# Gated complex attention and GEGLU on one core: more transposes by DMA, unread matmuls, float32 sums in the first units, wider gate blocks

## The chip, the cores and the metric

The kernel runs on one core of a Trainium2 chip. Its engines are TensorE (PE), VectorE (DVE), ScalarE (ACT), GpSimd (POOL) and SyncE (SP), which here only issues transfers. The metric is the device time of one execution in microseconds. A profile is one execution taken by the hardware profiler, and its time is a little longer than the median of the runs without it.

## The reference, cut to what matters

Inputs `q`, `k`, `v`, `a_re`, `a_im` have 4 batches, 8 heads, 768 positions and 48 elements. The first half is a linear attention whose state decays by a complex gate per position and element; the second half is a gated feed-forward block over 3072 tokens of 384 elements (8 heads x 48), with 1536 hidden elements.

```python
mag = np.sqrt(a_re * a_re + a_im * a_im)
scale = np.minimum(mag, 0.999) / (mag + 1e-06)
for t in range(S):
    new_re = ar * S_re - ai * S_im
    new_im = ar * S_im + ai * S_re
    S_re, S_im = (new_re + outer(k[t], v[t]), new_im)
    y[t] = q[t] @ S_re
x = y of all heads, 3072 x 384
val = x @ w_val;  gelu = GELU(x @ w_gate)
out = x + sigmoid(x @ w_res) * ((gelu * val) @ w_out)
```

The kernel does not step through the positions. It takes logarithm and angle of the gate, sums both over the 128 positions of a tile with a triangular matrix on PE, scales q by the exponential of the sum and k by its inverse, and turns both by cosine and sine of the summed angle. Scores inside a tile are then plain matmuls under a mask, and what comes from earlier tiles goes through a state of 96 x 48 a head.

## The kernel before, in words

**Units.** A tile is 128 positions of one batch, with all 8 heads. The 24 tiles are grouped into 14 units (lines 211 to 217): units 0 and 1 are one tile each, units 2 to 11 two tiles each, and units 12 and 13 one tile each. Unit 2 holds the first tiles of batches 2 and 3; from unit 3 on, two units take each next position tile of batches 0, 1 and 2, 3.

**Steps.** `prepare` (L364), `attend` (L512) and `forward` (L577) do not run anything; each adds steps to a plan, 1450 of them. `Plan.run` (L158) then issues them in the order of the hand-given list `ORDER` (an index per step), so that list sets the order on every engine's queue. Each engine works its own queue strictly in that order. `PLACE` says for steps that may run on several engines which one takes them. Buffers are given out in the same order: a step whose buffer is still in use waits for the last user. Where ACT changes between the tables for logarithm and exponential (L), for arctangent and sine (T) and for GELU and tanh (G), a table load is put in (L652). Steps of DVE and POOL that share a port wait for one another in turn (L179 to L183).

**Prepare, for one unit.** SP loads `ar`, `ai`, `q`, `k`, `vf` (L373), a transfer for each tile. ACT takes Ln of `ar` into `la` (L394) and Exp of its negative into `t` (L395); `t` times `ai` (L397) is the tangent; its square (L399 or L401) goes through Ln again (L402), and L403 joins both into the log magnitude. L406 caps it and rounds it to the short float format `lh`, L408 makes the rest `ll`; `sums` (L359) adds both up on PE with two matmuls into a bank, and ACT takes E and Ei, the exponentials of the sum and of its negative (L423, L424). ACT takes the arctangent (L433), the carry of the tile before is added by a DMA of POOL (L440, L446), `th` and `tl` are its two parts (L450, L452), summed by `sums` as well; ACT rounds the number of turns (L462) and DVE takes them off (L464). `fw` is the absolute value (L471 or L473), and two sines fill `CS` (L477). L482 scales q and k, L487 makes the features `fQ`, `fK` of 128 x 8 x 128. They are then transposed to `QT`, `KT`: in units 0 to 7 on PE (L504, eight matmuls against the identity for each tile and each of Q and K), with a copy out of the bank by DVE or ACT (L507); in units 8 to 13 (`PE_T = 8`) by a transposing DMA of SP (L496). L510 casts `v`.

**Attend.** Scores (L535), mask (L538), the product with v and the state (L547, L549), the copy `x` (L552), and the new state: L559, U (L565), Gb (L567) and Gf (L572).

**Forward.** `x` is transposed (on PE in units 0 to 2, L591; by DMA later, L583). For each pair of the 12 hidden blocks of 128, PE fills one bank with gate products and one with value products (L605); ACT takes the GELU of the gate bank (L610), and DVE multiplies it with the value bank (L611). A block of a unit with two tiles is 256 wide, so two blocks are 512 elements and fill a bank; in a unit of one tile, two blocks are 256 and fill half of it. L620 and L622 make the residual gate, L631 the output product, L635 and L638 the result, L640 the store.

**Memory.** PE writes into eight banks, all of one kind (`Bank`). The wide float32 buffers are a pool of 25 (`WD`), of which each unit takes 16: five loads, la, t, s, E, Ei, fr, fw, lh, ll, th, tl. The weights are loaded and cast by DMAs that POOL issues (L340), in the order 6 x wg, wr, 6 x wv, 3 x wo, between POOL's other work.

Of the kernel before, what the change touches and what calls it, by code (L numbers as in the profile page):

```python
# [9 lines left out]
FP = mybir.dt.float32  # L10
# [10 lines left out]
PE_T = 8  # L21
SL, ST = 1,1
WD = 25
# [7 lines left out]
    24: "DVE", 33: "DVE", 40: "DVE", 50: "DVE", 51: "ACT", 53: "ACT", 64: "ACT", 104: "POOL", 114: "ACT", 116: "POOL",  # L31
    132: "ACT", 145: "ACT", 190: "DVE", 191: "DVE", 203: "DVE", 213: "DVE", 223: "DVE", 225: "ACT", 236: "DVE", 252: "ACT",
    305: "DVE", 306: "DVE", 318: "DVE", 322: "ACT", 323: "POOL", 330: "DVE", 340: "DVE", 345: "DVE", 347: "ACT", 353: "DVE",
    422: "DVE", 435: "DVE", 438: "POOL", 446: "DVE", 460: "DVE", 463: "ACT", 551: "DVE", 554: "POOL", 555: "POOL", 562: "DVE",
    572: "DVE", 576: "DVE", 585: "DVE", 595: "DVE", 667: "DVE", 670: "ACT", 671: "POOL", 686: "ACT", 688: "DVE", 692: "DVE",
    771: "DVE", 786: "POOL", 787: "POOL", 821: "DVE", 866: "DVE", 872: "DVE", 899: "DVE", 902: "POOL", 903: "POOL", 910: "DVE",
    933: "DVE", 984: "DVE", 1014: "ACT", 1015: "POOL", 1050: "DVE", 1088: "DVE", 1121: "ACT", 1124: "POOL", 1125: "POOL",
    1151: "DVE", 1160: "DVE", 1198: "DVE", 1232: "POOL", 1233: "POOL", 1240: "DVE", 1251: "ACT", 1257: "DVE", 1304: "DVE",
    1325: "POOL", 1329: "DVE", 1344: "DVE", 1376: "DVE", 1396: "ACT", 1397: "POOL", 1410: "ACT", 1448: "DVE",
}  # L40
ORDER = [
    97, 98, 16, 102, 293, 17, 103, 410, 104, 21, 105, 22, 106, 294, 23, 24, 411, 179, 115, 295, 34, 35, 116, 296, 117, 107, 25,
    178, 118, 303, 26, 36, 420, 27, 37, 108, 119, 28, 100, 181, 180, 413, 304, 109, 120, 421, 110, 305, 121, 38, 29, 188, 30,
    111, 39, 306, 412, 307, 32, 99, 182, 189, 308, 112, 309, 190, 31, 125, 191, 319, 310, 101, 526, 41, 321, 122, 40, 19, 18,
    123, 320, 42, 113, 183, 299, 204, 422, 124, 205, 127, 130, 33, 527, 423, 436, 206, 43, 207, 528, 20, 529, 184, 44, 126, 314,
    192, 46, 128, 316, 193, 210, 45, 322, 208, 424, 194, 47, 195, 49, 211, 323, 131, 129, 199, 52, 196, 209, 48, 536, 315, 311,
    212, 324, 135, 425, 50, 537, 1, 185, 298, 137, 437, 54, 200, 132, 114, 138, 538, 312, 136, 198, 325, 313, 326, 426, 55, 327,
    300, 759, 297, 186, 758, 53, 7, 141, 56, 133, 197, 539, 139, 328, 643, 642, 213, 134, 201, 214, 51, 329, 60, 438, 140, 57,
    216, 439, 58, 144, 202, 2, 187, 330, 215, 334, 12, 552, 217, 8, 332, 553, 6, 0, 219, 331, 218, 226, 336, 142, 220, 768, 333,
    143, 222, 227, 145, 224, 62, 440, 761, 645, 644, 301, 302, 225, 335, 441, 223, 769, 554, 221, 242, 343, 443, 59, 555, 61,  # L50
    339, 243, 63, 240, 652, 64, 344, 444, 341, 233, 231, 442, 241, 228, 234, 317, 244, 445, 653, 146, 760, 337, 5, 342, 232,
    559, 540, 340, 874, 4, 654, 3, 245, 150, 235, 154, 560, 338, 556, 875, 561, 236, 85, 170, 360, 87, 152, 350, 156, 166, 203,
    345, 148, 361, 81, 354, 65, 171, 9, 10, 168, 446, 11, 83, 229, 162, 427, 73, 13, 164, 158, 77, 67, 75, 351, 417, 416, 160,
    557, 89, 355, 541, 79, 90, 69, 358, 74, 431, 558, 230, 71, 151, 318, 359, 770, 251, 364, 348, 365, 66, 155, 153, 349, 433,
    428, 432, 68, 362, 429, 14, 76, 363, 771, 430, 163, 655, 346, 82, 86, 70, 147, 84, 78, 347, 157, 656, 149, 249, 72, 165,
    167, 252, 159, 237, 172, 250, 884, 367, 15, 238, 357, 257, 91, 885, 88, 169, 269, 352, 80, 562, 542, 784, 447, 657, 92, 415,
    253, 239, 161, 448, 261, 543, 414, 273, 173, 366, 93, 353, 563, 564, 668, 877, 369, 174, 658, 450, 876, 434, 669, 254, 94,
    175, 368, 452, 263, 255, 449, 258, 265, 277, 259, 455, 986, 419, 418, 278, 451, 459, 267, 533, 988, 279, 256, 886, 785, 457,
    456, 275, 453, 458, 274, 280, 454, 1206, 370, 670, 435, 659, 372, 464, 374, 386, 460, 271, 671, 246, 465, 530, 382, 887,
    276, 260, 248, 1097, 388, 376, 390, 466, 461, 467, 384, 474, 476, 480, 544, 95, 1207, 392, 247, 531, 356, 475, 786, 547,  # L60
    270, 371, 468, 545, 532, 477, 548, 549, 787, 272, 469, 675, 1096, 772, 373, 262, 266, 281, 481, 987, 773, 546, 1216, 672,
    660, 534, 646, 989, 484, 535, 176, 676, 264, 268, 888, 550, 677, 478, 470, 788, 471, 479, 791, 566, 889, 663, 462, 662, 661,
    792, 96, 673, 282, 793, 287, 1106, 674, 375, 996, 568, 565, 288, 283, 463, 789, 665, 997, 485, 387, 567, 1107, 664, 647,
    473, 284, 177, 289, 391, 571, 575, 573, 377, 389, 285, 790, 900, 396, 394, 649, 648, 577, 290, 551, 678, 1098, 393, 486,
    998, 679, 572, 569, 286, 574, 680, 510, 570, 506, 487, 378, 764, 291, 576, 901, 681, 1208, 592, 650, 488, 774, 490, 511,
    397, 775, 1099, 502, 380, 492, 383, 590, 482, 683, 504, 498, 508, 591, 385, 593, 881, 651, 1306, 1209, 902, 582, 491, 999,
    395, 500, 903, 689, 379, 489, 586, 685, 381, 493, 483, 690, 1000, 594, 398, 583, 1108, 686, 776, 779, 907, 765, 595, 778,
    580, 587, 399, 581, 781, 780, 908, 1217, 596, 794, 601, 400, 904, 578, 682, 584, 472, 777, 880, 292, 1378, 684, 404, 905,
    597, 499, 1109, 579, 585, 909, 600, 1218, 687, 1311, 503, 688, 628, 691, 405, 762, 401, 763, 599, 666, 906, 1122, 696, 890,
    507, 692, 706, 795, 402, 698, 406, 505, 697, 501, 403, 693, 512, 699, 1379, 878, 1012, 589, 520, 610, 509, 1219, 796, 911,  # L70
    708, 494, 407, 1013, 618, 707, 408, 602, 709, 879, 614, 782, 598, 798, 513, 612, 629, 620, 992, 995, 1123, 604, 496, 1307,
    616, 495, 710, 700, 603, 766, 797, 891, 895, 767, 892, 619, 896, 799, 497, 1001, 521, 701, 893, 1383, 910, 716, 615, 800,
    1384, 711, 617, 1385, 1312, 894, 897, 605, 522, 783, 913, 1014, 514, 801, 611, 802, 810, 805, 898, 1313, 515, 806, 882, 717,
    1124, 523, 702, 607, 703, 621, 712, 516, 1015, 912, 1230, 613, 803, 606, 726, 804, 517, 1215, 899, 1002, 914, 993, 883, 994,
    990, 622, 1003, 608, 807, 728, 667, 588, 734, 811, 915, 808, 738, 730, 722, 991, 917, 736, 723, 916, 732, 624, 609, 814,
    623, 824, 713, 918, 740, 724, 815, 812, 822, 1314, 1016, 1004, 1213, 625, 813, 725, 825, 1220, 1006, 1019, 823, 1007, 727,
    694, 731, 524, 518, 1125, 809, 1033, 695, 1020, 1315, 729, 816, 1017, 525, 920, 919, 1021, 636, 817, 1018, 704, 1009, 1008,
    1005, 1316, 735, 1025, 519, 1102, 828, 718, 626, 637, 705, 720, 733, 737, 714, 926, 638, 1231, 1386, 832, 826, 1022, 639,
    719, 818, 630, 1026, 827, 627, 1308, 1210, 833, 1100, 927, 640, 715, 829, 1322, 721, 1129, 631, 1024, 936, 1126, 924, 937,
    641, 921, 632, 1394, 925, 1127, 739, 1232, 1130, 819, 633, 1381, 1023, 928, 1128, 929, 1028, 744, 752, 746, 934, 742, 747,  # L80
    753, 842, 1027, 1221, 1131, 1387, 1110, 741, 409, 831, 935, 1031, 1032, 1323, 1395, 844, 1309, 1030, 846, 754, 1132, 938,
    1222, 944, 939, 1317, 1111, 1112, 848, 743, 1223, 858, 834, 847, 1103, 836, 1113, 945, 745, 859, 1045, 838, 748, 930, 755,
    634, 835, 840, 1029, 1046, 849, 1324, 1114, 1047, 922, 830, 1212, 1048, 1133, 843, 1117, 1233, 1211, 1101, 635, 923, 931,
    1134, 837, 839, 1224, 950, 845, 1325, 1105, 1310, 749, 1038, 850, 1318, 1119, 1116, 1118, 841, 1319, 1115, 1136, 1104, 1320,
    1036, 1039, 946, 851, 966, 756, 1321, 1225, 1037, 1226, 1049, 757, 1135, 1380, 854, 972, 1050, 821, 852, 1214, 948, 853,
# [101 lines left out]
def kernel(  # L187
# [25 lines left out]
    if SPLIT:  # L213
        units[-SPLIT:] = [[x] for u in units[-SPLIT:] for x in u]
    NU = len(units)
    where = {bc: (p, i) for p, u in enumerate(units) for i, bc in enumerate(u)}
    size = [len(u) for u in units]

    ctx.enter_context(tc.manual_schedule())
# [463 lines left out]
```

## Time and profile before

| | |
|---|---|
| median of 3 runs | 261.19 us (261.1 to 262.1) |
| profiled execution | 262.78 us, span from first to last instruction 261.0 us, mean clock 0.978 |
| busy, share of the span | PE 226.4 us (87%), DVE 225.4 (86%), ACT 214.1 (82%), POOL 94.5 (36%) |
| ACT table loads (L652) | 36, 46.2 us |
| gate and value products (L605) | 1008, 115.1 us busy |
| output products (L631) | 288, 56.5 us busy |
| transposes of features on PE (L504) | 224, 20.1 us busy |
| transposing DMAs of QT, KT / of xT | 20 / 20 |
| first gate product, first GELU | 55.4 us, 59.1 us |

The page cuts the span into 40 slices of 6.5 us and gives the busy share of each engine in tenths; a view of stretches gives the same for any stretch in microseconds, with the clock that PE was granted. A timeline lists instructions in order of time: start, length, engine, line, operation, what is written and read, its shape and how many were merged into the row; in brackets the idle time ahead of it and what ended that. Lengths of matmuls are modelled and overlap, so the spacing of their starts is the better measure of what they cost. The chain of waits follows the end back through what released each step.

### The profile page before, as it was taken

What the parts mean: (1) busy time and instruction counts of PE and PEld (TensorE: products, weight loads), DVE (VectorE), ACT (ScalarE), POOL (GpSimd) and SP (SyncE); (2) the same over time, 40 slices, a digit from 0 to 9 for tenths busy, and PEclk for the clock granted to TensorE, in tenths of its full rate; (3) what the DMA queues carried; (4) which work ended last, traced back from release to release, by engine and by line L of the source; (5) the groups of instructions that cost most, each with busy time, mean ns of one, the idle gap of its engine ahead of it and who ended that gap; (6) DMA issues with size and microseconds to landing.
All of it is one profiled execution on the core that took longest, in us unless ns stands there. A gap on an engine that the chain in (4) does not pass through costs nothing.

```text
span 261.0 us, 6358 instructions
## 1 busy us (share of the span) xinstructions
PE 226.4 (87%) x2426; PEld 181.8 (70%) x2426; DVE 225.4 (86%) x404; ACT 214.1 (82%) x355; POOL 94.5 (36%) x114
## 2 busy tenths in 40 slices
PE   0230992889999999999999999999999999999993
PEld 0120772778978977877878877778778777887881
DVE  2589889999899999999999999999999794965363
ACT  4999999899899999999998999999988684241240
POOL 3013086196605743576625634351420001110110
PEclk9999996599999999999999999999999999999998
DMA  8999999989999997995989896999757919402111
GB/s 141 187 187 186 187 194 192 213 163 213 202 184 172 167 186 163 221 146 124 211 149 190 148 179 149 182 168 236 133 114 160 117 23 136 133 3 63 60 63 60
DMA packets 162174, 39.83 MB, mean 153 GB/s; under 512 B 155617, under 2 KB 162145, under 8 KB 162145
## 3 DMA queue, kind: packets, MB, share of 16 engines
q1 hardware_dynamic: 157696, 35.53, 79.4%
q0 software_dynamic: 4448, 3.90, 9.3%
q8 instruction: 19, 0.31, 0.5%
q14 instruction: 11, 0.08, 0.1%
HBM read 31.26 MB, written 4.72 MB: 138 GB/s over the span
## 4 chain that ended last, share of the span: by engine, by line
PE 71%; DMA 11%; ACT 9%; DVE 3%; POOL 2%; SPq 1%; issue 1%; POOLq 0%; DVEq 0%
PE pb L605 32%; PE pb L631 17%; PE pb L359 6%; PE pb L620 4%; PE pb L504 4%; PE pb L535 3%; DMA wo<-in_moe_w_out_dram 3%; DMA wv<-in_moe_w_val_dram 2%; DMA ai<-in_a_im_dram 2%; ACT L652 2%; DMA t<-fr 2%; DMA ar<-in_a_re_dram 2%; POOL t L397 1%; PE pb L549 1%; PE pb L547 1%; ACT CS L477 1%
## 5 line engine op out<-in xcount | busy, mean ns | idle before, releaser
L610 ACT ACTIVATE h<-pb 128x512 bf16<-128x512 f32 (+1 forms) x84 | 41.2, 547 | 23.2 <-PE pb L631 13.0
L605 PE MATMUL pb<-xT,wv 128*128 128x256 bf16 (+1 forms) x504 | 58.1, 257 | 0.4 <-DMA wv<-in_moe_w_val_dram 0.4
L605 PE MATMUL pb<-xT,wg 128*128 128x256 bf16 (+1 forms) x504 | 57.0, 257 | 0.0
L631 PE MATMUL pb<-wo,h 128*128 128x384 bf16 x288 | 56.5, 326 | 0.0
L611 DVE SCALAR_TENSOR_TENSOR h<-h,pb 128x512 bf16<-128x512 bf16 (+1 forms) x84 | 48.5, 602 | 4.2 <-PE pb L605 2.8
L605 PEld LDWEIGHTS <-wg 128*128 128x128 bf16 x504 | 42.9, 98 | 7.1 <-issue 0.8
L652 ACT ACT_TABLE_LOAD x36 | 46.2, 1283 | 1.3 <-PEq L667 0.7
L605 PEld LDWEIGHTS <-wv 128*128 128x128 bf16 x504 | 41.9, 98 | 7.5 <-issue 1.3
L638 POOL TENSOR_TENSOR ot<-ot,x 128x384 f32<-128x384 f32 x16 | 14.6, 913 | 65.0 <-DVE Gb L567 23.4
L631 PEld LDWEIGHTS <-h 128*128 128x128 bf16 x288 | 26.3, 97 | 13.0 <-issue 0.4
L538 DVE TENSOR_TENSOR am<-pb,mask 128x512 bf16<-128x512 f32 x48 | 31.9, 680 | 2.9 <-PE pb L535 2.8
L397 POOL TENSOR_TENSOR t<-t,ai 128x768 f32<-128x768 f32 (+1 forms) x10 | 16.0, 1601 | 18.1 <-DVE fK L487 9.0
L504 PE MATMUL pb<-ident,fK 128*128 128x128 bf16 x112 | 10.0, 246 | 13.5 <-DVE fK L487 13.5
L359 PE MATMUL pb<-th,ut_one 128*128 128x384 f32 x24 | 11.3, 471 | 11.4 <-POOL th L334 11.1
L452 POOL TENSOR_TENSOR tl<-t,th 128x768 fp32r<-128x768 f32 (+1 forms) x10 | 16.5, 1656 | 10.4 <-DVE ll L408 7.8
L635 DVE SCALAR_TENSOR_TENSOR ot<-sg,pb 128x384 f32<-128x384 f32 x24 | 13.1, 547 | 6.8 <-PE pb L631 5.0
L504 PEld LDWEIGHTS <-fK 128*128 128x128 bf16 x112 | 8.4, 112 | 15.0 <-DVE fK L487 14.3
L535 PE MATMUL pb<-QT,KT 96*128 96x128 bf16 x192 | 17.7, 225 | 0.5 <-DMA QT<-fQ 0.4
L535 PEld LDWEIGHTS <-KT 96*128 96x128 bf16 x192 | 13.8, 101 | 3.9 <-issue 2.2
L622 ACT ACTIVATE sg<-pb 128x384 f32<-128x384 f32 x24 | 11.6, 502 | 5.3 <-PE pb L620 2.8
L620 PE MATMUL pb<-wr,xT 128*128 128x384 bf16 x72 | 15.5, 326 | 0.0
L423 ACT ACTIVATE E<-pb 128x384 f32<-128x384 f32 x24 | 11.5, 500 | 3.2 <-PE pb L359 3.0
(91 smaller groups left out, 472.2 us busy)
## 6 DMA issues: line engine op xcount, KB each, us to landing
ar<-in_a_re_dram SPq DMA_DIRECT2D x24, 192.0 KB, 4.6
ai<-in_a_im_dram SPq DMA_DIRECT2D x24, 192.0 KB, 4.6
k<-in_k_dram SPq DMA_DIRECT2D x24, 192.0 KB, 4.4
q<-in_q_dram SPq DMA_DIRECT2D x24, 192.0 KB, 4.5
vf<-in_v_dram SPq DMA_DIRECT2D x24, 192.0 KB, 4.3
out_dram<-ot SPq DMA_DIRECT2D x24, 192.0 KB, 2.8
wg<-in_moe_w_gate_dram POOLq DMA_DIRECT2D x6, 192.0 KB, 5.6
wv<-in_moe_w_val_dram POOLq DMA_DIRECT2D x6, 192.0 KB, 5.9
```

The costliest lines, as they stand in the source:

```text
L359: nc.tensor.matmul(out=bank.tile, lhsT=ut_one, rhs=x[:, i * DM:(i + 1) * DM], start=(j == 0), stop=(j == 1))
L397: add(e1, "tai", lambda: on[e1].tensor_tensor(out=F("t"), in0=F("t"), in1=flat(T("ai"), n), op=OP.mult), [s["ai"]], [s["t"]], n)
L452: add(e10, "tl", lambda: on[e10].tensor_tensor(out=F("tl"), in0=F("t"), in1=F("th").bitcast(FP), op=OP.subtract), [s["t"], s["th"]], [s["t ...
L504: nc.tensor.transpose(out=tp.tile[:, h, :], in_=s[g].tile[:, i * H + h], identity=ident)
L535: nc.tensor.matmul(out=ap.tile[:, h, :], lhsT=kT.tile[0:DD, u * H // 2 + h, :], rhs=qT.tile[0:DD, u * H // 2 + h, :], start=True, stop=True)
L538: add("DVE", "am", lambda u=u, am=am, ap=ap: nc.vector.tensor_tensor(out=am.tile[:, u * H // 2:(u + 1) * H // 2, :], in0=ap.tile, in1=mask ...
L605: nc.tensor.matmul(out=o_.tile[:, u, :], lhsT=w_[:, k_, (2 * m + u) * 128:(2 * m + u + 1) * 128], rhs=s["xT"].tile[:, k_, 0:n].rearrange(" ...
L610: add("ACT", "gelu", lambda gp=gp, hv=hv: nc.scalar.activation(out=hv(), in_=gp.tile, func=AF.Gelu), [gp], [hh], n, "G")
L611: add("DVE", "h", lambda vp=vp, hv=hv: nc.vector.scalar_tensor_tensor(out=hv(), in0=hv(), scalar=0.5, in1=vp.tile, op0=OP.mult, op1=OP.mul ...
L620: nc.tensor.matmul(out=rp.tile, lhsT=s["xT"].tile[:, k_, i, :], rhs=wr[:, k_, :], start=(k_ == 0), stop=(k_ == KF - 1))
L631: nc.tensor.matmul(out=op_.tile, lhsT=s["h2"].tile[:, k_, i * 128:(i + 1) * 128], rhs=wo[:, k_, :], start=(k_ == 0), stop=(k_ == NF - 1))
L652: plan.run(ORDER, lambda table: nc.scalar.preload_act_table_set(ACT_SETS[table]), after)
```

## The change

- `PE_T` goes from 8 to 6: units 6 and 7 get their `QT` and `KT` by transposing DMAs of SP.
- `PF_L = PF_T = 4`: in units 0 to 3 the log magnitude and the angle are not split. DVE caps the log magnitude in float32, and one float32 matmul with the triangular matrix `ut_f` makes each sum; `lh`, `ll`, `th`, `tl` are not made there.
- 18 steps (`WARM`) are put in, each eight 128 x 128 products of the identity with itself into a bank that nothing reads.
- A bank takes `w = 512 // (n * 128)` hidden blocks, so four in units 0, 1, 12 and 13, and two as before in the others.
- `ar` is loaded straight into `la`, and Ln works in place, so each unit takes one wide buffer less (and units 0 to 3 five less). la, t, s, fr, fw come from a class `Quad`, which may hold four tiles; with `QUAD = 14` and 14 units every group is one unit, so the four-tile case does not arise.
- Gb after the first tile may be placed on POOL, and 11 of 16 are.
- `PLACE` and `ORDER` are new throughout: 1400 steps instead of 1450 (the 18 unread ones included), in another order on every engine.

Instructions by engine, where the counts differ: PE loses 64 transposes and 12 x 2 halves of split sums, and gains 12 float32 sums and 144 unread products (96 ahead of the first gate product, 48 behind it). ACT has 38 table loads instead of 36, 12 GELU over 512 elements for 24 over 256, and 5 evictions of QT and KT instead of 8; DVE has 15 instead of 20. POOL's order of weights is wg, wg, wg, wg, wv, wg, wg, wr, wv x5, wo x3. SP issues 28 transposes of QT and KT instead of 20.

```diff
-PE_T = 8
-SL, ST = 1,1
-WD = 25
+PE_T = 6
+PF_L, PF_T = 4, 4
+WD, WQ = 25, 5
+CSB = 2
+QUAD = 14
+WARM = 18
...
+        act("ln", lambda: nc.scalar.activation(out=A("la"), in_=A("la"), func=AF.Ln), [], allv("la"), "L", N4)
...
+        if p >= PF_L:
+            add("DVE", "lh", ...)
+            add("DVE", "ll", ...)
         else:
+            add("DVE", "cap", lambda: nc.vector.tensor_scalar(out=PF("la", p), in0=PF("la", p), scalar1=LOG_CAP, scalar2=0.0,
+                                                              op0=OP.min, op1=OP.add), [], [V["la"][p]], n)
...
+            if p >= PF_L:
+                add("PE", "cumL", lambda i=i: sums(clm[i], i, F("lh"), F("ll")), [s["lh"], s["ll"]], [clm[i]])
             else:
+                add("PE", "cumL4", lambda i=i: nc.tensor.matmul(out=clm[i].make([128, DM]), lhsT=ut_f, rhs=P("la", p)[:, i],
+                                                               start=True, stop=True), [V["la"][p]], [clm[i]])
...
-        for m in range(NF // 2):
+        w = 512 // (n * 128)
+        for m in range(NF // w):
...
-                    o_.make([128, 2, n * 128])
-                    for u in range(2):
+                    o_.make([128, w, n * 128])
+                    for u in range(w):
                         for k_ in range(KF):
...
     weights()
-    for p in range(NU):
-        prepare(p)
-        attend(p)
-        forward(p)
+    for _ in range(WARM):
+        wb = Bank()
+
+        def f(wb=wb):
+            wb.make([128, 512])
+            for _ in range(8):
+                nc.tensor.matmul(out=wb.tile[:, 0:128], lhsT=ident, rhs=ident, start=True, stop=True)
+        add("PE", "warm", f, (), [wb])
+    for grp in groups:
+        prepare(grp)
+        for p in grp:
+            attend(p)
+            forward(p)
```

## The prediction

> **What bounds the kernel now.** I read the busy table and the slices first, then stretches of ten and seventy microseconds, then the timelines of PE and ACT around the point where the gate blocks begin. On the page, in the slices, PE is nearly empty up to about 55 us and full from then on; ACT and DVE are full until about 200 us and then thin out; DMA is full for 190 us.
>
> ```profile
> PE   0230992889999999999999999999999999999993
> DVE  2589889999899999999999999999999794965363
> ACT  4999999899899999999998999999988684241240
> DMA  8999999989999997995989896999757919402111
> ```
>
> The stretches say the same in microseconds (columns: length, busy time and instructions of PE, PE weight loads, DVE, ACT, POOL, then clock, DMA share, GB/s):
>
> ```profile
> 20.00:30.00 10.00, 3.50 (x19) 2.60 (x20) 9.00 (x17) 9.43 (x13) 2.36 (x3) 1.00 1.44 186
> 40.00:50.00 10.00, 4.69 (x58) 4.24 (x58) 9.90 (x16) 9.21 (x12) 5.23 (x8) 0.56 1.24 208
> 60.00:130.00 70.00, 69.53 (x815) 57.74 (x813) 68.18 (x121) 68.09 (x115) 38.73 (x40) 1.00 1.04 180
> 200.00:257.00 57.00, 56.69 (x618) 44.60 (x616) 39.36 (x78) 25.31 (x48) 4.15 (x5) 1.00 0.39 77
> ```
>
> A busy PE need not be a PE at its peak, so I counted. Spacing in the timeline gives what a matmul costs when nothing is late: 128x256 gate 0.109 us (12 in 1.31), 128x128 0.0557 (16 transposes in 0.89), 128x384 output or residual 0.163 (4 in 0.65), 128x48 0.026, one half of a split sum 0.175, a small M product 0.27. The first residual matmul (L620) starts at 58.70, and in program order from there stand 720 x 0.109 + 264 x 0.0557 (narrow gate) + 360 x 0.163 + 294 x 0.0557 (transposes, L535) + 464 x 0.026 + 64 x 0.175 + 9 x 0.27 = 193.8 us. The last matmul ends at 256.7, which is 198.0 later: **only 4.2 us of those 198 are lost**. So from 58.7 on PE's own work is the bound, and the end is when the gate phase starts + PE work left + 4.2 + a tail of 4.3 (256.7 to 261.0: the last addition and store). Ahead of it ACT bounds: it is 92 to 99% busy from 10 to 60 us, and the first gate block can leave its bank only when ACT comes to the first GELU:
>
> ```profile
> 57.26 0.51 ACT L462 ACTIVATE fr<-pb 128x384 int32<-128x384 f32 x1
> 57.79 1.28 ACT L652 ACT_TABLE_LOAD   x1
> 59.09 1.21 ACT L610 ACTIVATE h<-pb 128x256 bf16<-128x256 f32 x4
> ```
>
> **ACT up to the first GELU.** The changed order has 8 table loads ahead of it as before, but 77 instructions instead of 83. With the mean durations of this profile: removed, moved to DVE and POOL or put later are two copies of KT (2.0), three of x (1.5), two of v (1.0), two of xT (0.95), two roundings (1.0), a th (0.85), one narrow fw and one narrow square (1.0), 8.3 in all; added are four E and Ei (2.0), a QT (1.0), a wide Ln (0.95), a wide square and a wide fw (1.7), 5.65. **That is -2.7 us**: first GELU at 56.4. DVE, in the same way, has 60.3 us of instructions ahead of its first h before and 56.2 after, so it does not take the place of ACT: what it gains (two xT, two more x) is less than the ll, th, tl it loses.
>
> **Float32 sums.** In units 0 to 3, six tiles and two sums each, one float32 matmul takes the place of a pair of split ones: 12 matmuls for 24, and four ll on DVE (0.55 and 0.95 each, 3.0) and th and tl of four units go. All 12 stand ahead of the first gate matmul. No row shows a 128x384 float32 product; between a pair of passes like the split rows (0.35) and four bf16 rows (0.65), twice that at half clock. I take 0.65; PE idles 10.1 us ahead of 26.0 there, so this lies beside ACT's work and counts nothing. Uncovered, the range is no loss to 12 x (1.3 - 0.64) = +8 us; the saved th and tl steps could give 1 us back.
>
> **Unread products.** 96 of the 144 stand ahead of the gate phase; at 0.0557 to 0.107 they are 5 to 10 us in a PE that has some 26 idle there. 48 stand behind it, in the full PE: 2.7 us, counted in full. If they fill the waits that are part of the 4.2, they cost nothing.
>
> What they can give: at 31.92 eight transposes were spaced as sixteen are at 81.15,
>
> ```profile
> 31.92 1.06 PE L504 MATMUL pb<-ident,fK 128*128 128x128 bf16 x8
> 81.15 1.06 PE L504 MATMUL pb<-ident,fK 128*128 128x128 bf16 x16
> ```
>
> so PE ran at half speed then, whatever the clock row says, and again from 40 to 50, where the granted clock was 0.56. The chain of waits runs through PE from 29.3 to 35.7, six microseconds that would be three. I count none of it, since ACT was 98% busy there and had other steps to run; the bound on this side is -3.0. The Trainium skill (TensorE: Matmul & The Clock Gate, Part 1) says that half clock is the default, that some 3.4 us of sustained work releases it and an idle window of that length brings it back; by that rule the products would earn those 3.0 us and the sum below would be 251.7.
>
> **Two more units by DMA.** Units 6 and 7 lose 64 transposes (3.6 us of the full PE, at 110 to 145 us) and eight evictions (0.68 on DVE or 1.0 on ACT); SP gains eight transposes at 1.3 us of issue and 3.4 to 3.8 us to landing. SP waits for other engines some 108 us in all, and no engine waited over 2.4 us for a transpose, so I take this as hidden; not hidden it is up to 8 x 1.3 = 10.4.
>
> **Four gate blocks a bank.** Units 0, 1, 12, 13: 24 GELU of 396 ns become 12 of 607 (-2.2 on ACT), 24 products of 414 ns become 12 of 677 (-1.8 on DVE). No PE work is saved, but five blocks of 12 matmuls, not four of 6, fit in the banks ahead of the first residual matmul: 36 narrow matmuls (2.0 us) move out of the full stretch into the earlier one. In the whole kernel DVE loses some 10 us and ACT 9 (11 Gb go to POOL, two table loads come), so neither becomes the bound.
>
> **The sum.** From the first residual matmul the changed order has 720 x 0.109 + 228 x 0.0557 + 360 x 0.163 + 214 x 0.0557 + 464 x 0.026 + 64 x 0.175 + 9 x 0.27 + 48 x 0.0557 = 190.0, 3.8 less (2.0 + 4.5 - 2.7; of the 4.5, 3.6 are the transposes and 0.9 are 16 scores now done earlier). It starts 2.7 earlier if PE reaches it as ACT reaches the GELU, as before. Together -6.5: 56.0 + 190.0 + 4.2 + 4.3 = 254.5 of span, and with the 1.8 us around the span (262.78 against 261.0) 256.3. The median of the runs shown, 261.19, is 1.6 below the profiled run; the forecast goes by the median: 261.19 - 6.5 = 254.7, say **254.7**.
>
> **Rivals.**
> 1. *The transposes delay the loads* (slower). All transfers of SP stand in one queue behind each other; DMA share is 1.04 from 60 to 130 and 0.89 to 200, with 192-byte runs nearly throughout (155617 of 162174 packets are under 512 B). If loads come just in time there, eight transposes push them by 10.4 us: 254.7 + 10.4 = 265.1. It decides once a load lands after its first reader is ready; above 6.5 us of such lateness the gain is gone. Against it: today the largest wait for a load past 60 us is 0.4 us, and the float32 units and the load of a_re straight into la free buffers, so loads can start earlier. The Trainium skill (DMA: Bandwidth & Descriptors, Issuing engines are not separate DMA queues) speaks for it: all queues share the same 16 DMA engines; the saturated share above agrees.
> 2. *The start does not move.* If the weights bound it (the chain ends at wv landing at 64.2 and wo at 77.4), only the transposes less the late products count: 3.6 - 2.7 = 0.9, so 260.3. For it: both waits are in the chain. Against: PE waited 0.4 us for wv.
> 3. *The products and float32 sums are not covered* at half clock: 10.3 + 7.9 us more PE time with 16 us of room ahead of the first transposes; I price the overflow at 3: 257.7.
> 4. *The lost time goes too.* An earlier start and a lighter ACT and DVE take away the 4.2: 250.5.
>
> **Chances.** Forecast (252 to 259) 0.54; rival 4, with the full clock at the start, 0.18; rival 3 0.08; rival 2 0.08; rival 1 0.12. Range: from 249 (rival 4 and a little of the -3.0) to 261 (rivals 2 and 3 in); the slower one, at 265, stays out with part of the fastest. A measurement of this kernel can tell about 0.5%, 1.3 us, from no change: faster 0.8 (forecast, 3, 4), same 0.08 (rival 2), slower 0.12.
>
> **What would show it.** First GELU near 56.4; PE work from the first residual matmul within 5 us of its elapsed time; 160 transposes on PE instead of 224, none for units 6 and 7; clock 1.0 from 40 to 50. I am wrong if PE shows idle time past 70 us with QT, KT or a load as releaser (rival 1), if the first GELU stays near 59 (2), or if ACT idles on sums before 40 us (3).

## The result, and the profile after

The changed kernel takes **264.67 us** (median of 4 runs) against 261.35 for the kernel before (4 runs beside them): a ratio of 1.0114, 95% interval 1.0070 to 1.0158. The forecast was 254.7 with a range of 249 to 261. Its profiled execution took 264.79 us, with a span of 263.0.

The slices of the page after look like those of before, but for PE's start and one thin slice past 60 us:

```profile
PE   4098645977899999999999999999989999999993
DVE  2559898995999999799999999999989693855434
ACT  5799999997799999899999979796998782224230
DMA  8999999999999999978998997999989793500202
```

The stretches that the prediction showed, now of the changed kernel (length, then busy time and instructions of PE, PE weight loads, DVE, ACT, POOL, then clock, DMA share, GB/s):

```profile
20.00:30.00 10.00, 7.38 (x65) 4.68 (x62) 9.91 (x22) 9.74 (x16) 3.98 (x6) 1.00 1.39 188
40.00:50.00 10.00, 7.33 (x92) 6.66 (x93) 9.23 (x14) 9.97 (x13) 6.58 (x10) 0.70 1.22 194
60.00:130.00 70.00, 67.41 (x771) 54.28 (x769) 66.19 (x112) 65.12 (x105) 34.98 (x38) 1.00 1.01 179
200.00:257.00 57.00, 56.81 (x617) 45.71 (x616) 35.97 (x64) 24.83 (x44) 7.64 (x9) 1.00 0.45 89
```

From 60 to 130 us PE is busy for 67.4 us, where it was 69.5, and DVE and ACT are 2 to 3 us emptier. Nobody is full there any more. So something else held all three. The first GELU comes earlier, as forecast, but by 1.5 us and not by 2.7 (59.09 to 57.56), and behind it ACT stops:

```profile
56.27 1.28 ACT L736 ACT_TABLE_LOAD   x1
57.56 0.60 ACT L685 ACTIVATE h<-pb 128x512 bf16<-128x512 f32 x1
58.06 0.49 ACT L539 ACTIVATE fr<-pb 128x384 int32<-128x384 f32 x1
58.43 1.66 ACT L685 ACTIVATE h<-pb 128x512 bf16<-128x512 f32 x3
61.70 0.84 ACT L446 ACTIVATE s<-t 128x768 f32<-128x768 f32 x1 [1.61 <-POOL t L443]
```

The bracket names POOL's product `t` x `ai` of unit 7. POOL's own timeline of the changed kernel tells what that waited for:

```profile
59.86 1.81 POOL L443 TENSOR_TENSOR t<-t,ai 128x768 f32<-128x768 f32 x1 [2.25 <-DMA ai<-in_a_im_dram]
...
63.58 0.82 POOL L361 CAST v<-vf 128x768 bf16<-128x768 f32 x1 [1.38 <-DMA vf<-in_v_dram]
```

DVE's timeline shows who waited with ACT:

```profile
61.70 0.96 DVE L528 TENSOR_TENSOR tl<-t,th 128x768 fp32r<-128x768 f32 x1 [2.10 <-POOL t L443]
```

and PE's who waited for DVE:

```profile
62.71 0.44 PE L386 MATMUL pb<-tl,ut_one 128*128 128x384 f32 x1 [1.28 <-DVE tl L528]
```

SP's timeline has the issues of these loads (start, time that the issue took):

```profile
45.74 5.72 SPq L416 DMA_DIRECT2D vf<-in_v_dram  x2
51.50 3.15 SPq L416 DMA_DIRECT2D ai<-in_a_im_dram  x1
54.69 0.70 SPq L416 DMA_DIRECT2D vf<-in_v_dram  x1
```

SP issues the load of `ai` only at 51.5, because the loads ahead of it have not gone out, and it lands at 59.7. Buffers were not what held them: by the plan's own rule for buffers, the last user of every buffer that the loads issued between 40 and 55 us write had ended by 39.0 (that of this `ai` by 32.2). SP's list of waits puts 3.2 us in this stretch down to DVE's copy into `QT`, which uses none of these buffers. POOL waits for `ai`. DVE's `tl` of unit 5 needs nothing of unit 7, but takes its turn at the shared port behind POOL (the port order of the plan), and waits 2.1 us. ACT's square of unit 7 stands ahead of a GELU and of the residual's tanh, and holds them 1.6 us. PE waits 1.3 us for `tl`. One late load stops four engines.

**The account.** With the prediction's spacings, PE work from the first residual matmul is 190.0 us, the forecast. But that matmul starts at 60.1 and not at 56.0 (before: 58.7), and 8.9 us are lost behind it, not 4.2; the tail is 4.0. 60.1 + 190.0 + 8.9 + 4.0 = 263.0. The same thing as PE work still to come (matmuls from that time on, times their spacing, unread products left out):

| PE work left at | 50 us | 60 | 70 | 100 | 130 | 200 | last matmul ends |
|---|---|---|---|---|---|---|---|
| before | 199.8 | 192.4 | 183.4 | 153.9 | 124.7 | 56.2 | 256.7 |
| changed | 194.1 | 187.3 | 180.8 | 152.7 | 125.3 | 58.2 | 259.0 |
| changed, long runs in its loads (below) | 192.9 | 185.1 | 176.5 | 147.6 | 119.7 | 51.4 | 252.1 |

At 50 us the changed kernel is 5.7 us ahead. It gives back 2.5 between 60 and 70, another 2.7 for the unread products (the last of them at 132 us), and the rest in many small waits.

### The profile page after: what moved, and what is told of

Its sections match the earlier page's. It is cut to its first block, busy times and chain, and to the rows that moved or that the text cites. A ratio compares the mean times of both kernels' runs of the same rounds, so it can differ in the third digit from the quotient of the medians.

```text
span 263.0 us, 6488 instructions
## 1 busy us (share of the span) xinstructions
PE 233.3 (89%) x2506; PEld 184.1 (70%) x2506; DVE 218.3 (83%) x376; ACT 207.4 (79%) x334; POOL 97.3 (37%) x121
## 2 busy tenths in 40 slices
DMA packets 170623, 41.95 MB, mean 159 GB/s; under 512 B 164064, under 2 KB 170592, under 8 KB 170592
## 4 chain that ended last, share of the span: by engine, by line
PE 58%; DMA 12%; ACT 9%; DVE 9%; SPq 8%; issue 3%; POOL 0%; DVEq 0%; ACTq 0%; POOLq 0%
PE pb L680 28%; PE pb L706 13%; SPq L416 7%; PE pb L695 4%; DMA vf<-in_v_dram 3%; PE pb L386 3%; DMA xT<-x 3%; PE pb L608 2%; DMA t<-fr 2%; DMA k<-in_k_dram 2%; PE pb L577 2%; DMA ai<-in_a_im_dram 2%; ACT CS L462 2%; ACT L736 1%; PE pb L632 1%
## 5 line engine op out<-in xcount | busy, mean ns | idle before, releaser
L685 ACT ACTIVATE h<-pb 128x512 bf16<-128x512 f32 x72 | 40.6, 611 | 29.6 <-PE pb L680 18.9
L680 PE MATMUL pb<-xT,wg 128*128 128x256 bf16 (+1 forms) x504 | 56.4, 257 | 1.4 <-DVE am L611 0.7
L680 PE MATMUL pb<-xT,wv 128*128 128x256 bf16 (+1 forms) x504 | 56.4, 257 | 0.7 <-DVE fr L541 0.6
L686 DVE SCALAR_TENSOR_TENSOR h<-h,pb 128x512 bf16<-128x512 bf16 x72 | 47.3, 678 | 6.1 <-PE pb L680 5.8
L713 POOL TENSOR_TENSOR ot<-ot,x 128x384 f32<-128x384 f32 x17 | 15.5, 912 | 55.3 <-issue 13.8
L443 POOL TENSOR_TENSOR t<-t,ai 128x768 f32<-128x768 f32 (+1 forms) x11 | 17.5, 1591 | 14.2 <-ACT t L440 6.5
L361 POOL CAST v<-vf 128x768 bf16<-128x768 f32 (+1 forms) x11 | 8.1, 736 | 29.3 <-DVE fQ L560 6.0
L537 PE MATMUL pb<-t,ut_f 128*128 128x384 f32 x12 | 6.5, 645 | 9.9 <-ACT t L452 9.0
L520 POOL DMA_DIRECT2D t<-fr x12 | 10.7, 953 | 11.7 <-DVE x L361 4.4
L497 POOL DMA_DIRECT2D mr<-E x11 | 8.6, 786 | 17.1 <-ACT E L493 17.1
L646 POOL TENSOR_TENSOR Gf<-U,M 96x384 f32<-96x384 f32 x10 | 8.2, 824 | 16.4 <-DVE ll L479 9.4
```

What stands on the lines that cost most here:

```text
L443: add(e1, "tai", lambda p=p, e1=e1: on[e1].tensor_tensor(out=PF("t", p), in0=PF("t", p), in1=flat(st[p]["ai"].tile, size[p]), op=OP.mult), ...
L680: nc.tensor.matmul(out=o_.tile[:, u, :], lhsT=w_[:, k_, (w * m + u) * 128:(w * m + u + 1) * 128], rhs=s["xT"].tile[:, k_, 0:n].rearrange(" ...
L685: add("ACT", "gelu", lambda gp=gp, hv=hv: nc.scalar.activation(out=hv(), in_=gp.tile, func=AF.Gelu), [gp], [hh], 2, "G")
L686: add("DVE", "h", lambda vp=vp, hv=hv: nc.vector.scalar_tensor_tensor(out=hv(), in0=hv(), scalar=0.5, in1=vp.tile, op0=OP.mult, op1=OP.mul ...
L713: add(e8, "otx", lambda i=i, ot=ot, e8=e8: on[e8].tensor_tensor(out=ot.tile, in0=ot.tile, in1=s["x"].tile[:, i].rearrange("p h d -> p (h d ...
```

## The experiments

Each time is a median, and each ratio is to the kernel before on the same chip in the same session (it had 262.3 to 262.6 there). The changed kernel's own ratio is 1.0114.

**Theories.** A: the parts work as priced, the new order's waits between engines lose the gain. B: the parts themselves bring the waits. From what the first pair of kernels showed came C: the loads cannot come earlier than they do, so an order that needs them earlier waits for them.

### The order or the parts

```diff
 # constants of the changed kernel; ORDER and PLACE from the kernel before: steps of both keep
 # their place, a float32 sum takes that of the split one, a wide gate step that of the first of
 # its two narrow ones, a transfer of QT or KT stands right behind its feature step
-WARM = 18
+WARM = 0
-ORDER = [ 34, 100, 101, ...
+ORDER = [ 82, 83, 16, ...
```

> The changed kernel's parts (transposes of units 6 and 7 by DMA, float32 sums in units 0 to 3, four gate blocks a bank in one-tile units, ar loaded straight into la) with the order and the engine placement of the kernel before; no unread products. Theory A, the parts do what was predicted and the new order loses it: PE work from the first residual matmul is lower by 3.6 us or more and waits stay near the 3.0 us of before, so 255 to 259 us. Theory B, the parts themselves bring the waits (transposes push loads, float32 sums hold PE): 261 us or more.

276.78 us, ratio 1.0562 (1.0533 to 1.0591). A is out in this form: the parts in the old order are far slower.

```diff
-PE_T = 6
-PF_L, PF_T = 4, 4
-WARM = 18
+PE_T = 8
+PF_L, PF_T = 0, 0
+WARM = 0
 # new order kept; transposes a dozen steps behind the transfers that they replace
```

> The changed kernel's order and placement with three parts undone: units 6 and 7 transposed on PE again, split sums in units 0 to 3, no unread products; the four gate blocks a bank and the in-place load stay. Theory A (the new order is what loses): it keeps the waits and gets back 3.6 us of transposes but loses the 2.7 us of late products, so 264 to 269 us. Theory B (the parts lose): 259 to 262 us.

272.74 us, ratio 1.0380 (1.0353 to 1.0407). B is out too: with three of the parts undone (four blocks a bank and the load straight into `la` stay) the new order is 7 us slower than with them. First gate product: 58.8, against 53.2. Parts and order belong together; neither explains the result alone.

```diff
-            for _ in range(8):
+            for _ in range(0):
                 nc.tensor.matmul(out=wb.tile[:, 0:128], lhsT=ident, rhs=ident, start=True, stop=True)
```

> The changed kernel with the 144 unread products left out, their places in the order kept. If the 48 late ones cost what was predicted: 2.7 us less, 262 us. If they stand in waits: no difference, 264.5 us. If the early ones earn clock at the start (granted clock or spacing of matmuls ahead of 50 us gets worse without them and the first GELU comes later): 266 us or more.

263.44 us, ratio 1.0025 (1.0000 to 1.0049): 0.9% or 2.3 us less than the changed kernel, near the 2.7 forecast; the intervals nearly touch. First gate product 53.5 and first GELU 57.8, so up to the first GELU the early products bring 0.3 us at most.

```diff
 # ORDER: 748 is POOL's t x ai of unit 7, 537 DVE's tl of unit 5, 749 ACT's square of unit 7
-84, 156, 424, 398, 10, 748, 537, 90, 229, 11, 749, 158, ... 333, 542, 81,
+84, 156, 424, 398, 10, 537, 748, 90, 229, 11, 158, ... 333, 542, 749, 81,
```

> The changed kernel with two steps moved: POOL's product t x ai of unit 7 goes behind DVE's tl of unit 5, and ACT's square of unit 7 behind the last rounding of unit 5. Theory A: the 2.1 us in which DVE waits for POOL's turn, POOL itself waiting for the load of ai, go, with ACT's 1.6 and PE's 1.4 beside them, so 262 to 263 us. Rival: the next late thing, the load of vf of unit 3 that lands at 63.5, takes their place, so 264 to 265 us.

268.01 us, ratio 1.0204 (1.0161 to 1.0247), above both expectations. PE's wait for `tl` went, but PE's longest wait past 50 us is now for `v` (total, times, longest):

```profile
PE pb L622 <- POOL v L363: 1.1, 1, 1.1
```

POOL's timeline shows why: the moved product waits for its turn behind `tl`, and the cast of `v` of unit 3 stands behind it.

```profile
60.99 1.81 POOL L445 TENSOR_TENSOR t<-t,ai 128x768 f32<-128x768 f32 x1 [2.96 <-DVE tl L530]
62.76 0.57 POOL L369 DMA_DIRECT2D wv<-in_moe_w_val_dram  x1
63.33 0.83 POOL L363 CAST v<-vf 128x768 bf16<-128x768 f32 x1
```

The last `vf` of unit 3 had landed at 62.2. So the cast gained 0.2 us on the changed kernel (63.58), which waited there for `vf` itself: behind one late load stood another, and the turn was only the first to show. Why the whole got some 2 us slower than the changed kernel is open; PE's waits over 0.15 us past 50 us add up to 5.7 instead of 4.8.

### The loads

```diff
-nc.sync.dma_start(out=tile()[:, i], in_=src[b, :, c * 128:(c + 1) * 128, :].rearrange("h t d -> t h d"))
+nc.sync.dma_start(out=tile()[:, i].rearrange("p h d -> p (h d)"),
+    in_=src.rearrange("b h s d -> (b h s) d").rearrange("(t p g) d -> t p (g d)", p=128, g=8)[b * NC + c])
```

Done in both kernels: as many bytes, in runs eight times as long (1,536 bytes instead of 192). The inputs are regrouped by it, so these kernels leave out the right order of the positions and heads and their output is not the reference's; instructions and order stay.

> The kernel before, but each of the 120 input loads takes 128 runs of 1,536 consecutive bytes instead of 1,024 runs of 192, so the inputs are regrouped and the output isn't the reference's; bytes, instructions and order are the same. If the transfers bound the stretch up to 70 us (their DMA share is over 1.0 there), it drops and the kernel gets 3 us or more faster: 258 or less against 261.4. If ACT and DVE bound it: 260.5 to 261.5.

261.66 us, ratio 0.9954 (0.9924 to 0.9984). The kernel before gains 1.2 us; its first gate product stays (55.5 against 55.4). Loads do not bind it.

> The changed kernel with the same long runs in its loads. Theory C (the gain at the start was lost to loads that land late: ai of unit 7 at 59.9, vf of unit 3 at 63.5): with loads early, the change is worth what was predicted, some 6 us less than before_long_runs, so 252 to 256. Theory A (the new order's waits on engines, not on loads, lose it): it stays 1 to 3 us slower than before_long_runs.

257.82 us, ratio 0.9803 (0.9762 to 0.9844): **the changed kernel gains 8 us** (0.9803 against 1.0114), and is 1.5% or 3.9 us faster than the other one with long runs. That is C, though not in full: C forecast some 6 us and 252 to 256. The stretches 0 to 60 and 60 to 70 us of the four kernels follow (columns as above). The kernel before:

```profile
0.00:60.00 60.00, 30.54 (x260) 23.53 (x261) 48.34 (x88) 54.29 (x87) 24.84 (x39) 0.91 1.24 183
60.00:70.00 10.00, 9.57 (x162) 8.56 (x160) 8.98 (x19) 8.74 (x22) 5.65 (x7) 1.00 1.21 209
```

The changed kernel:

```profile
0.00:60.00 60.00, 37.80 (x386) 28.77 (x386) 46.54 (x84) 54.02 (x82) 24.87 (x40) 0.94 1.20 182
60.00:70.00 10.00, 7.91 (x118) 6.25 (x116) 7.55 (x13) 7.50 (x13) 4.66 (x5) 1.00 1.21 207
```

The kernel before with long runs:

```profile
0.00:60.00 60.00, 27.95 (x258) 21.26 (x259) 48.34 (x88) 54.17 (x87) 25.19 (x40) 0.89 0.73 197
60.00:70.00 10.00, 10.00 (x174) 9.23 (x172) 9.65 (x22) 9.34 (x24) 5.72 (x7) 1.00 1.10 194
```

The changed kernel with long runs:

```profile
0.00:60.00 60.00, 39.32 (x411) 30.38 (x412) 49.13 (x89) 55.74 (x87) 28.41 (x43) 0.94 0.79 208
60.00:70.00 10.00, 9.75 (x160) 8.50 (x159) 9.97 (x19) 9.27 (x15) 3.75 (x6) 1.00 0.78 105
```

Read the last two columns. With 192-byte runs the share is 1.2 in both kernels, and they move the same 182 to 183 GB/s. In all thirteen versions with these runs, in whatever order, 44 to 46 of the 120 loads have landed by 60 us, at 177 to 186 GB/s and shares of 1.13 to 1.24. With long runs it is 50, and 197 to 208 GB/s need a share of only 0.73 to 0.79. From 60 to 70 us the changed kernel's DVE is busy for 9.97 us instead of 7.55. PE's waits past 50 us in the changed kernel with long runs shrink to three:

```profile
PE pb L620 <- DVE v L361: 0.8, 1, 0.8
PE pb L680 <- DVE am L611: 0.7, 1, 0.7
PE pb L680 <- DVE fr L541: 0.2, 1, 0.2
```

The Trainium skill (DMA: Bandwidth & Descriptors, the table at its start) gives 512 bytes as the least for full rate; the shares above agree, 192-byte runs needing 1.5 to 1.7 times the share for fewer bytes. From 40 to 66 us of the changed kernel SP's transfers take 64.1% of the 16 DMA engines' time and POOL's, with the weights, 51.6%. So the weights may gain room as well: the pair shows that the transfers bind, and not which of them.

**What is left with early loads.** The sum of the prediction for the two kernels with long runs: 58.8 + 193.9 + 3.1 + 4.3 = 260.1 before, 57.9 + 190.1 + 4.1 + 4.0 = 256.1 changed. PE work is 3.8 lower, as forecast, and 4.1 are lost. But the first residual matmul starts only 0.9 sooner and not 2.7, although the first GELU comes 3.9 sooner (55.3 against 59.2). PE's timeline of the changed kernel with long runs, from its first gate product to that matmul (the rows between left out):

```profile
50.56 1.50 PE L680 MATMUL pb<-xT,wg 128*128 128x128 bf16 x24
...
53.92 0.36 PE L620 MATMUL pb<-v,am 128*128 128x48 bf16 x8 [0.83 <-DVE v L361]
...
55.86 0.83 PE L680 MATMUL pb<-xT,wg 128*128 128x128 bf16 x12 [0.72 <-DVE am L611]
...
57.85 1.14 PE L695 MATMUL pb<-wr,xT 128*128 128x384 bf16 x6
```

In the new order 60 narrow gate products stand between, not 24, with scores, sums and two waits for DVE beside them: 7.3 us, where the kernel before has 3.3 (55.4 to 58.7).

```diff
 # ORDER of no_products: 174, 287, 286 load vf of units 2 and 3; 739, 738 load ai of unit 7
-33, 739, 317, ... 206, 174, 407, ... 320, 287, 212, ... 80, 738, 326, 146, 426, 286, 12,
+33, 174, 287, 286, 739, 738, 317, ... 206, 407, ... 320, 212, ... 80, 326, 146, 426, 12,
 # and 748 behind 327 (POOL's cast of v of unit 3), 749 behind 542
```

> The changed kernel without the 144 unread products, with real inputs, and with six steps moved: the last three loads of vf of units 2 and 3 go ahead of both loads of ai of unit 7, POOL's t x ai of unit 7 goes behind its cast of v of unit 3, ACT's square of unit 7 behind the last rounding of unit 5. If it is these loads that hold the start: PE's waits of 60 to 70 us go and the time is 258.5 to 261 (no_products was 262.0 at the same base). If any reordering only makes another load late, since the transfers are full up to 66 us: 262 or more.

265.03 us, ratio 1.0090 (1.0059 to 1.0121), slower than no_products with the same work. Another order of the same loads did not help, as C has it, but this is no clean test: `vf` of unit 3 landed at 56.1, and POOL's cast of it still stood idle until 61.2, in turn behind DVE's `tl` of unit 5, which ended at 61.1. In no_products the cast ran at 60.8.

### Each part, with late loads and with early ones

The transposes back on PE (`PE_T = 8`), then the split sums back (`PF_L = PF_T = 0`), in the new order; then both again with the long runs, and no_products too. The steps put back stand at places chosen by hand in an order made without them; so this is what taking a part out costs, and not what an order made for the rest would reach.

```diff
-PE_T = 6
+PE_T = 8
```

> The changed kernel with units 6 and 7 transposed on PE again: 64 transposes and 8 evictions come back, 8 transposing DMAs go, each at the place in the order a few steps behind. By the prediction 3.6 us of PE work comes back: 268 us. If the transposing DMAs cost as much in late loads as they save: 263 to 265 us. If they cost more: below 263.

267.89 us, ratio 1.0173 (1.0130 to 1.0216): 0.6%, 1.5 us, more than the changed kernel, though the intervals overlap.

```diff
-PF_L, PF_T = 4, 4
+PF_L, PF_T = 0, 0
```

> The changed kernel with split sums in units 0 to 3 again (lh and ll in place of the cap, th and tl on DVE ahead of the angle's sums, two halves for each float32 matmul). By the prediction the float32 sums lie beside ACT's work and count nothing either way: 264 to 266 us. If the four steps that they save on DVE set the start: first GELU 2 to 5 us later and 267 to 270 us. If the float32 matmuls hold PE: 262 us.

268.94 us, ratio 1.0220 (1.0180 to 1.0259): 2.8 us more, first gate product 5.8 us later (59.0). ACT's waits up to 60 us in this kernel show why; the first was 0.3 us in the changed kernel:

```profile
ACT fr L554 <- PE pb L401: 4.1, 2, 2.2
ACT la L454 <- DMA la<-in_a_re_dram: 4.0, 2, 2.1
ACT CS L477 <- DVE fr L556: 1.7, 1, 1.7
```

> after_long_runs with units 6 and 7 transposed on PE again (regrouped inputs). If the DMA transposes save what was predicted once loads are early: 3.6 us more, 261.4. With late loads it was only 1.5 us more; if that holds here too: 259.3.

261.69 us, ratio 0.9976 (0.9948 to 1.0003): 4.5 us more than after_long_runs, where the forecast had 3.6.

> after_long_runs with split sums in units 0 to 3 again (regrouped inputs). If it is DVE's four steps and their place that set the first gate product (5.8 us later with late loads): the first gate product comes 5 us later again and the time is 261 to 263. If the float32 sums only gained because loads were late: 258 to 259.

264.68 us, ratio 1.0087 (1.0056 to 1.0118): 7.4 us more, above the expectation, with the first gate product 6.4 later.

> after_long_runs without the 144 unread products (regrouped inputs, so not the reference's output). With the loads out of the way PE is the bound, so the 48 late products should cost their full 2.7 us: 255.0 to 255.5 against 257.8; if the 96 early ones earn clock, part of it is lost: 256 to 257.8.

257.73 us, ratio 0.9829 (0.9781 to 0.9877), against 0.9803: no difference that shows, where 2.7 us had been expected. So by these medians the transposes and the float32 sums are worth two to three times as much with early loads as with late ones, though the 1.5 us is hardly clear of noise; only the products cost nothing there.

### Each part alone in the old order

These three have the kernel before's order and placement, made as for parts_old_order, with one part each; all three load `ar` straight into `la`.

```diff
 # float32_alone          # transposes_alone       # four_blocks_alone
 PE_T = 8                 PE_T = 6                 PE_T = 8
 PF_L, PF_T = 4, 4        PF_L, PF_T = 0, 0        PF_L, PF_T = 0, 0
 w = 2                    w = 2                    w = 512 // (n * 128)
```

> The kernel before, order and placement as they were, with float32 sums in units 0 to 3 alone (and ar loaded straight into la). By the forecast nothing, 261.5. If these sums set the start in any order, as in the new one: first gate product 2 us or more earlier and 256 to 260. If they hold PE or their buffers upset the loads: 263 or more.

263.45 us, ratio 1.0014 (0.9978 to 1.0050): nothing. First gate product 55.7, although transposes already ran at 0.057 us apiece at 30 us.

> The kernel before, order and placement as they were, with units 6 and 7 transposed by DMA alone, each transfer placed right behind the feature step (and ar loaded straight into la). By the forecast 3.6 us less: 258. If SP's queue holds the transfers or what stands behind them, as between 120 and 151 us of parts_old_order: 265 to 272.

272.48 us, ratio 1.0348 (1.0292 to 1.0404). At 100 us it had 5.2 us less PE work left than the kernel before, 3.6 of them the transposes. Then PE waited for what SP's one queue brought. PE's timeline:

```profile
120.08 0.66 PE L710 MATMUL pb<-wr,xT 128*128 128x384 bf16 x3 [1.79 <-DMA xT<-x]
...
124.74 0.61 PE L623 MATMUL pb<-QT,KT 96*128 96x128 bf16 x4 [3.35 <-DMA KT<-fK]
```

SP's timeline, in which a transpose of `x` stands behind two of `KT`:

```profile
119.91 3.64 SPq L584 DMA_TRANSPOSE KT<-fK  x2
123.64 1.22 SPq L672 DMA_TRANSPOSE xT<-x  x1
```

> The kernel before, order and placement as they were, with four gate blocks a bank in the one-tile units alone, each wide step at the place of the first of its two narrow ones (and ar loaded straight into la). By the forecast no PE work saved, 4 us of ACT and DVE saved: 259 to 261.5. If twelve matmuls in one step hold PE's order: 263 or more.

268.07 us, ratio 1.0189 (1.0143 to 1.0236). A block of four reaches over the middle of the 12 hidden blocks, so it needs all six loads of `wv` where two needed three, and PE took them one by one, as its timeline shows (2.7 us of the 5):

```profile
64.66 0.23 PE L694 MATMUL pb<-xT,wv 128*128 128x128 bf16 x1 [0.79 <-DMA wv<-in_moe_w_val_dram]
65.88 0.23 PE L694 MATMUL pb<-xT,wv 128*128 128x128 bf16 x1 [0.99 <-DMA wv<-in_moe_w_val_dram]
67.05 0.23 PE L694 MATMUL pb<-xT,wv 128*128 128x128 bf16 x1 [0.94 <-DMA wv<-in_moe_w_val_dram]
```

The three single losses, 0.1, 3.5 and 1.9%, add up to 5.5%, about the 5.6% of parts_old_order: that run was slow through its transposes and its four blocks.

```diff
+LATE_WARM = {2, 4, 6, 8, 13, 14}
-            for _ in range(8):
+            for _ in range(0 if y in LATE_WARM else 8):
```

> The changed kernel with the 96 unread products ahead of the first gate product, without the 48 behind it. By the forecast 2.7 us less than the changed kernel, the same as no_products: 1.001 to 1.004 of the kernel before. If the 48 fill waits: 1.010 or more, and what no_products gained came from the early 96 or from the loads' chance.

264.74 us, ratio 1.0056 (1.0019 to 1.0092): between no_products and the changed kernel, telling them from neither.

## Why the prediction was wrong

**The step that failed** is the one in the sum: "It starts 2.7 earlier if PE reaches it as ACT reaches the GELU, as before", with the 4.2 us of lost time kept. It rested on the argument against rival 1: "today the largest wait for a load past 60 us is 0.4 us, and the float32 units and the load of a_re straight into la free buffers, so loads can start earlier". The first half is true of the kernel before, and says nothing of what happens once the readers come sooner; the second put the limit at the buffers. What held the loads was the transfers' own rate, 182 to 183 GB/s at a share of 1.2, in plain sight in the DMA column that the prediction showed. I read "waits for loads are small" as "loads have room". The first residual matmul came 1.4 later and not 2.7 earlier, and 8.9 us were lost. Shown by the pair with long runs: 8 us of the changed kernel's time, 1.2 of the other's.

**A second flaw in the same step** shows with the loads out of the way: the start is then 0.9 earlier. The sum tied the first residual matmul to the GELU "as before", and also moved 36 narrow products and 16 scores (2.9 us) ahead of that matmul, as if they took no time there. (This is read off the timelines; no run moves that work back.) So of the 6.5 us forecast, 3.9 come with early loads; of the 2.6 missing, 1.8 are this start, and 0.7 are lost time less tail (1.0 more lost than the kernel before with long runs, 0.3 less tail).

**Rivals.** Rival 1 had the right resource (loads late, slower than before) and the wrong agent, so its 265.1 comes near the 264.67 by luck: the loads that were late at 59.7 and 63.4 stand far ahead of the eight transposes in SP's queue, the first of which is issued at 113.7. Taking these out made the kernel slower still (1.0173), though by 1.5 us and not by the 3.6 of PE work that came back, so some 2 us may be theirs further on. They add 2.1 MB (41.95 against 39.83 on the page), and from 130 to 200 us the DMA share is 1.04 instead of 0.89. Rival 2 was right in that the first residual matmul does not come sooner, but the first GELU did move, and no wait of PE for `wv` over 0.15 us shows past 50 us. Rival 3's sign is not there: ahead of 40 us ACT waits 0.3 us for a float32 sum. Rival 4 went the other way, the lost time doubled.

**Term by term.**
- *First GELU, -2.7*: measured -1.5; ACT's work ahead of it fell by 1.8, its idle time rose from 5.7 to 6.0. With long runs it is -3.9 against the kernel before with long runs.
- *PE work, -3.8*: measured -3.8. Counting instructions by their spacing was safe.
- *Lost time, kept at 4.2*: measured 8.9. Of this the turn behind the load of `ai` is 1.3 at 61.4, and 0.6 at 68.7 is a wait for DVE, which had stood for 2.1 us. With early loads it is 4.1.
- *Float32 sums, nothing*: the price, 0.65, was right at full speed, where two passes of 0.32 make a product; the first ones ran at half speed, at 1.28. (The 645 ns in the group on the page are the mean length of one pass.) In the old order the sums are worth nothing (1.0014). In the new order they are worth 2.8 us, with early loads 7.4; with the split sums back and late loads, ACT waits 4.1 us for them. What hides a step is a property of the order, and the order changed.
- *Unread products, 2.7 in full*: between 0 (long runs) and 2.3 (no_products). PE's waits longer than 0.15 us past 50 us add up to 3.3 without them and 1.8 with them under long runs, so part of them stands in waits there. With late loads the profiles differ in more than the products: the same `ai` of unit 7 landed at 59.7 in the changed kernel and at 56.4 in no_products, the last `vf` of unit 3 at 63.4 and 60.0, with SP's order the same. One profile of each cannot say whether the products did that.
- *The bound of -3.0 for the clock*: not seen. Float32 sums alone brought full speed to the transposes from 28.8 us in the old order, and the first gate product did not move. The 251.7 by the Trainium skill's rule (TensorE: Matmul & The Clock Gate, Part 1) has no support here, though the rule on the clock itself fits: the granted clock kept a value for 3.4 us or multiples of it (in the kernel before 1.0 from 37.8 to 41.2, 0.5 to 51.4, then 1.0).
- *Two units by DMA, hidden*: 3.6 us was the price; it was 1.5 with late loads and 4.5 with early ones, and in the old order a loss of 9.1. Hidden only where the order had left room in SP's queue.
- *Four blocks a bank*: the 2.0 us of narrow gate products did move forward (60 ahead of the first residual matmul, not 24), but into a stretch where PE had to do them: from the first gate product to that matmul it took 6.9 us instead of 3.3. Narrow blocks in the new order were not tried.

The prediction also read PE as nearly empty up to 55 us. Its own slices have nines between 26 and 39, and PE is busy for 30.5 of the first 60 us; the sum does not rest on it.

**What stays open.** Why the products cost 2.3 us in one pair and nothing in the other, why 1.0 us more is lost with early loads, and how much of the changed kernel's loss of 2.3 us past 70 us (8.1 of lead lost in all, less 3.1 up to 70 and 2.7 of products) comes from the 2.1 MB more and how much from lateness carried on. No version tried beats the kernel before with its real loads; without the unread products the changed one is level with it (1.0025).

## What to carry to other kernels

In this kernel's first 60 us, at a DMA share of 1.2, as many loads landed whatever the order. So before counting an earlier start in such a stretch, list the loads that it needs and divide their bytes by the rate of that stretch. Small waits for loads in the present order are no slack. Work moved ahead of a point still takes its time there: do not count that point as earlier too. And a step's price "hidden" or "in full" holds for one order; test a part by taking it out of the new order, with the suspected bound lifted in both kernels.

## What the runs showed of the hardware

Float32 sums woke PE, not the unread products. In the changed kernel the first products ran at 0.106 us apiece at 1.5 us; the float32 sums went from 0.64 us a pass at 15.9 to 0.35 at 20.1 (a product is two passes, x4 below is two products), and the sixteen transposes at 28.3 were at full speed, 0.058 apiece. In the kernel before transposes reached that at 51.7 only; in the changed one they fell back once more, to 0.103 at 41.6 (clock 0.5 from 39.1 to 46.0). PE's timeline in the changed kernel:

```profile
13.20 2.93 PE L537 MATMUL pb<-t,ut_f 128*128 128x384 f32 x4 [8.99 <-ACT t L452]
15.92 2.77 PE L491 MATMUL pb<-la,ut_f 128*128 128x384 f32 x4
18.48 0.90 PE L537 MATMUL pb<-t,ut_f 128*128 128x384 f32 x2
...
28.34 1.09 PE L577 MATMUL pb<-ident,fK 128*128 128x128 bf16 x16 [0.44 <-DVE fK L560]
```

Without the products (no_products) full speed came at about 18 us as well, by the same float32 sums (0.32 a pass at 18.3), though it fell back to half at 28.4 for 3.4 us, where the changed kernel's did not. None of it moved the first gate product by more than 0.3 us (53.2, without the products 53.5; in the old order 55.4, with float32 sums alone 55.7). The clock column says 1.00 ahead of the trace's first record of the clock (37.8 us in the kernel before), whatever the spacing says: transposes at 26.0 were 0.103 apart there. The other surprise is how far the length of a run goes: the same 192 KB of a load, in runs of 1,536 bytes instead of 192, took the share of the first 60 us of the changed kernel from 1.20 to 0.79 while more bytes moved.
